# Scores and transposes on smaller tiles of the matmul array, and two weight halves loaded and split later

## The chip, the core and the metric

The kernel runs on one core of a Trainium2 chip. TensorE (PE in the profile, with its weight loads as PEld) multiplies, VectorE (DVE), ScalarE (ACT) and GpSimd (POOL) work elementwise, SyncE (SP) issues most of the DMAs. SBUF is the working memory with 128 partitions, PSUM the memory into which TensorE accumulates. The metric is the device time in microseconds, the median of the runs shown.

## The reference, cut to what matters

Three stages follow one another: a decayed linear attention, a mixture of experts with one expert for each token, and a feed-forward layer with a rational activation.

```python
def _attn_ref(q, k, v):                       # B=2, H=8, S=768, D=64
    gamma = 1.0 - 2.0 ** (-5.0 - np.arange(H)); scale = 1.0 / np.sqrt(D)
    for t in range(S):
        state = gamma[None, :, None, None] * state + np.einsum('bhd,bhe->bhde', k[:, :, t], v[:, :, t])
        y[:, :, t] = scale * np.einsum('bhd,bhde->bhe', q[:, :, t], state)

def _moe_ref(x, w_gate, w1, w2, capacity):    # x: 1536 x 512, 8 experts, hidden 1024
    logits = x @ w_gate; expert_idx = np.argmax(logits, axis=1)
    # gate_w: softmax weight of the chosen expert; each expert takes at most `capacity` tokens, in order
    h = np.maximum(np.einsum('ecd,edf->ecf', disp, w1), 0.0)
    y = np.einsum('ecf,efd->ecd', h, w2)      # out[i] = gate_w[i] * y[expert, place]

def _moe2_ref(x, w_in, w_out, a, b):          # 512 -> 2048 -> 512
    h = x @ w_in
    g = (a[0] + a[1]*h + a[2]*h**2 + a[3]*h**3) / (1 + |b[0]|*|h| + |b[1]|*h**2 + 1e-6)
    return g @ w_out
```

## The kernel before

**Attention** works on 12 units of 128 tokens (`u` = 0 to 11, six for each batch row), all eight heads of a unit at once. For one unit: `scores(u)` (L286) multiplies keys with queries into the PSUM tile `sc`, for each head a 64-row contraction that gives 128 keys x 128 queries; `mask(u)` (DVE, L294) multiplies by the causal mask into `scm`; `inter(u)` (L314) adds what the state of the earlier units gives into `yt`, as 64x64 tiles; `intra(u)` (L332) adds the masked scores times the values into the same `yt`, as 128x64 tiles; `attn_xt(u)` (DVE, L343) applies the decay and gives `xt`; `state(u)` (L300) accumulates keys times values, and ACT copies it out. `gate_mm(u)` (L352) multiplies each quarter of `xt` by the identity and the router's weights side by side (`wi`, 136 columns): that transposes 128 features into token order and gives the four parts of the logits. ACT copies the logits (`lgs`) and the tokens (`xs`), and SP stores the tokens to DRAM (`xd`). Matmuls written through `mm` have the line L341.

The loop over units (L619) writes each engine's order by hand: in a unit stand the scores of the next unit, `inter`, `intra`, `state`, and the `gate_mm` of the unit before. `sc` has one buffer, so the scores of a unit wait for the mask of the unit before.

**Routing** is done for two groups of units, 0 to 6 and 7 to 11. For the first group `gate_parts` (maximum, one-hot), `rank_mm` and `rank_pos` (places within an expert), `rank_put` (`pe`, `rr`) and `place_mm` (matmuls `tp` that put the tokens' numbers into slots) are spread over units 7 to 10, on DVE between the masks; for the second they stand behind the loop in `attn_tail` (L697), end in `indices` (`gidx`), and GpSimd then gathers the tokens of the first expert from `xd`.

**Expert weights** arrive in halves of 512 KB. A half is loaded into a raw buffer (`raw`, six of them), ACT copies it to a rounded part (`whi`, L143) and DVE forms the remainder (`wlo`, L148). Ten halves are requested inside the attention loop. Four tables (L36 to L39) say in which unit: `LOADS` the number of loads that SP issues, `HI_AT` which halves ACT copies, `LO_AT` which remainders DVE forms at a unit's start (before the mask of the next unit), `LO_END` which at its end. Halves 0 to 3 are the first expert's first layer, halves 4 to 7 its second.

**Behind the attention** the first expert works with the tokens of slot 0 already there (`early_x`, gathered by `early_gather` inside unit 10) and then with the tokens gathered last (`expert_x`, L891, matmuls `tp` at L899). Experts 1 to 7 and the feed-forward layer follow, with TensorE busy nearly throughout.

`warm` (L280) issues matmuls on zeros while TensorE has nothing to do: 7 before the first scores, 3 behind them.

Of the kernel before, what the change touches and what calls it, by code (L numbers as in the profile page):

```python
# [7 lines left out]
F32 = mybir.dt.float32  # L8
F32R = mybir.dt.float32r
# [23 lines left out]
DEC0 = 10  # L33
LAG = (2, 3, 4, 5)
WA, WC = 7, 3
LOADS = (0, 1, 0, 1, 0, 1, 0, 2, 1, 1, 1, 2)  # L36
HI_AT = {4: (0,), 5: (1,), 8: (2,), 9: (3, 4), 10: (5,)}
LO_AT = {6: (0,), 7: (1,)}
LO_END = {9: (2,), 10: (3,), 11: (4,)}  # L39
NA = 48  # L40
LOAD_AT = {1: (34, 0), 2: (34, 1), 6: (35, 0), 7: (35, 1)}
DEC_STEPS = (14, 15, 16, 17, 18, 19, 21, 22, 25, 26, 27, 28, 29, 30, 31, 33)
# [38 lines left out]
class Build:  # L81
# [198 lines left out]
    def warm(self, n, tag="tpa"):  # L280
        ps = self.bank(tag, "wp")
        for _ in range(n):
            rhs = self.wu.unsqueeze(1).to_broadcast([128, 4, 128])
            self.nc.tensor.matmul(ps, lhsT=self.wu, rhs=rhs, start=True, stop=True)

    def scores(self, u):  # L286
        kt, qt = self.feats(u)
        sc = self.sc[u] = self.pair_bank("s", "sc").rearrange("p (r j t) -> p r j t", r=2, j=4)
        for j in range(4):
            for r in range(2):  # L290
                rows = slice(64 * r, 64 * r + 64)
                self.mm(sc[:, r, j], kt[rows, j], qt[rows, j], True, True)

    def mask(self, u):  # L294
        m = self.col("mask").unsqueeze(1).to_broadcast([128, 8, 128])
# [56 lines left out]
    def gate_mm(self, u):  # L352
        nc = self.nc
        xt = self.xt.pop(u)
        if u < NU - 1:
            banks = [self.bank(t, "xk") for t in ("lg", "xk")]
        else:
            y = self.pair_bank("y", "xk")
            banks = [y[:, 0:512], y[:, 512:]]
        self.xk[u] = [b[:, 0 : 2 * 136].rearrange("p (k n) -> p k n", k=2) for b in banks]  # L360
        for k in range(4):
            nc.tensor.matmul(self.xk[u][k // 2][:, k % 2], lhsT=xt[:, k], rhs=self.wi[:, k], start=True, stop=True)
        for half in range(2):
            out = self.lgs[:, u, 2 * half : 2 * half + 2]
            nc.scalar.activation(out=out, in_=self.xk[u][half][:, :, 128:], func=AF.Copy)
# [205 lines left out]
    def attention(self):  # L571
        nc, tc, a = self.nc, self.tc, self.a
        with ExitStack() as st:
# [11 lines left out]
            self.xg0 = self.ap.tile([128, DM], F32, name="xg0")  # L585
            self.x0 = [self.ap.tile([128, 4, 128], F32R, name=n) for n in ("xh0", "xl0")]
            self.wu = self.ap.tile([128, 128], BF16, name="wu")
            nk = self.cols["gk"][0]
            self.attn_load(0, 0)
            nc.sync.dma_start(out=self.ca[:, 0:nk], in_=a["ct"][:, 0:nk])  # L590
# [11 lines left out]
            nc.sync.dma_start(out=self.ca[:, n1:], in_=a["ct"][:, n1:n0])  # L602
            dve, pool = nc.vector, nc.gpsimd
            dve.memset(self.wu, 0.0)
            dve.memset(self.ones, 1.0)
            self.warm(WA)
            self.scores(0)
# [4 lines left out]
            self.scale(1, pool)  # L612
            self.y_table(1, pool)
            self.y_table(2, pool)
            self.warm(WC)
            ident = self.col("ident").unsqueeze(1).to_broadcast([128, 4, 128])
            wg = self.col("wg").rearrange("p (k e) -> p k e", e=E)
            done = {GROUPS[b + 1] - 1: b for b in range(len(GROUPS) - 1)}
            for u in range(NU):  # L619
                last = u == NU - 1  # L620
                if u + 4 < NU:
                    for c in range(2):
                        self.attn_load(u + 4, c)
                self.load_next(LOADS[u])
                if u + 2 < NU:
                    self.scale(u + 2, pool)
                if u + 3 < UPB:
                    self.y_table(u + 3, pool)
                for n in LO_AT.get(u, ()):
                    self.split_lo(n // 2, n % 2)  # L630
# [37 lines left out]
                if u:  # L668
                    self.gate_out(u - 1, (1,))
                for n in HI_AT.get(u, ()):  # L670
                    self.split_hi(n // 2, n % 2)
                if u - 2 in done and not last:
                    self.rank_pos(done[u - 2])
                if u - 3 in done and not last:
                    self.rank_put(done[u - 3])
                for n in LO_END.get(u, ()):
                    self.split_lo(n // 2, n % 2)
# [19 lines left out]
    def attn_tail(self):  # L697
        u, b = NU - 1, len(GROUPS) - 2
        self.early_x()
        self.gate_mm(u)  # L700
        self.early_lo()
        ps = [self.pair_bank("s", "l1")[:, 0:512]]
        self.win_l1(self.x0, ps, range(0, 10))
        self.gate_group(b)
        self.gate_out(u)
        ps.append(self.pair_bank("y", "l1")[:, 0:512])
        self.load_next(4)
        self.rank_mm(b)
        self.rank_pos(b)
        self.h0 = self.wp.tile([128, 2, 512], F32, tag="wt", name="h0", bufs=3)  # L710
        self.split_hi(3, 0)
        self.win_l1(self.x0, ps, range(10, 12))
        self.win_relu(ps, self.h0, 0)
        self.split_hi(3, 1)
        self.rank_put(b)
        self.count()
        self.split_lo(2, 1)
        self.win_l1(self.x0, ps, range(12, 24))
        self.win_relu(ps, self.h0, 1)
        t0 = self.win_turn(self.h0, 0, self.bank("tpa", "htp"))  # L720
        self.place_mm(b, self.pair_bank("s", "tp"))
        t1 = self.win_turn(self.h0, 1, self.bank("st", "htp"))
        self.indices(self.gidx, E * (self.nsub + 1))
        self.split_lo(3, 0)
        self.ht0 = self.win_parts(t0)
        self.split_lo(3, 1)
        self.ht1 = self.win_parts(t1)
        self.overfull()
        self.nprep = 8
# [610 lines left out]
```

## Time and profile before

| what | value |
|---|---|
| median of 3 runs | 519.93 us (519.87 to 520.26) |
| the profiled execution | 519.19 us, of which span 517.4 us |
| TensorE busy | 504.2 us, 97% of the span |
| mean granted TensorE clock | 0.990 |
| attention loop, about | 4 to 59 us from the span's start |
| behind it to the first gathered tokens | 59 to 75 us |

A row of the timeline gives the start in us from the span's start, the time to the end of the last instruction merged into it, the engine, the line, the operation, what is written and read, the tile of the array in use (rows*columns) and the sizes; xN is the number of merged instructions. In square brackets stand the idle time of the engine before it and who ended that. Each fp32 matmul of the program shows as two passes. A pass of TensorE overlaps the next, so the difference of two starts tells what a group costs, and the length of a row is longer than that.

### The profile page before, as it was taken

How to read it: one execution, taken by the hardware profiler on the slowest of the kernel's cores; microseconds unless marked ns; L12 is line 12 of the kernel's file. 1: busy time of each engine (PE TensorE's matmuls, PEld its weight loads, DVE VectorE, ACT ScalarE, POOL GpSimd, SP SyncE). 2: the span in 40 equal slices, each digit the busy share in tenths (PEclk: the TensorE clock that was granted, in tenths of full speed). 3: DMA queues.
4: the chain of work that ended last, by engine and by line, in shares of the span. 5: the costliest groups of instructions: out<-in, count | busy, mean ns of one | idle time of the engine just before them, and what ended most of it. 6: DMA issues, size and time to landing. Idle time of an engine off the chain costs nothing.

```text
span 517.4 us, 9416 instructions
## 1 busy us (share of the span) xinstructions
PE 504.2 (97%) x3538; PEld 442.2 (85%) x3538; DVE 403.4 (78%) x578; ACT 362.0 (70%) x588; POOL 244.1 (47%) x187
## 2 busy tenths in 40 slices
PE   7999979999999999999999999999999999999995
PEld 5888857999999999999988888888888888888884
DVE  3468753897887979786596989999899998865973
ACT  1345515877685867755697989999899987776760
POOL 2531040023331548153454546776667865445775
PEclk9999989999999999999999999999999999999998
DMA  8999761989977999994310002222022200000203
GB/s 318 405 415 366 216 224 39 300 292 306 323 267 272 366 284 302 295 277 165 104 60 1 0 2 82 82 81 82 1 81 86 79 1 0 1 0 0 83 21 143
DMA packets 27554, 83.08 MB, mean 161 GB/s; under 512 B 4976, under 2 KB 5360, under 8 KB 27504
## 3 DMA queue, kind: packets, MB, share of 16 engines
q1 hardware_dynamic: 24880, 75.09, 43.0%
q0 software_dynamic: 2624, 7.35, 4.0%
q8 instruction: 28, 0.46, 0.4%
q14 instruction: 22, 0.18, 0.1%
HBM read 71.93 MB, written 10.49 MB: 159 GB/s over the span
## 4 chain that ended last, share of the span: by engine, by line
PE 64%; DVE 1%; POOL 1%; issue 1%; ACT 1%; POOLq 0%; DVEq 0%
PE h L1046 8%; PE h L1048 8%; PE h L1047 8%; PE o L1119 7%; PE o L1118 7%; PE o L1117 7%; PE l L928 3%; PE l L930 3%; PE l L957 3%; PE l L929 3%; PE l L956 3%; PE l L955 3%; POOL out L1148 1%; PE tp L899 1%; DVE fw L1083 0%
## 5 line engine op out<-in xcount | busy, mean ns | idle before, releaser
L148 DVE TENSOR_TENSOR wlo<-raw,whi 128x1024 fp32r<-128x1024 f32 x80 | 109.8, 1387 | 14.3 <-ACT whi L143 14.0
L1097 POOL TENSOR_TENSOR gg<-fx,gg 128x512 fp32r<-128x512 f32 x47 | 61.2, 1302 | 70.0 <-issue 62.2
L143 ACT ACTIVATE whi<-raw 128x1024 fp32r<-128x1024 f32 x80 | 83.2, 1055 | 3.5 <-PE l L956 3.4
L1046 PE MATMUL h<-yh,whi 128*128 128x512 f32 x192 | 74.9, 390 | 0.0
L1117 PE MATMUL o<-whi,gg 128*128 128x512 f32 x192 | 74.8, 390 | 0.0
L1047 PE MATMUL h<-yl,whi 128*128 128x512 f32 x192 | 74.7, 389 | 0.0
L1048 PE MATMUL h<-yh,wlo 128*128 128x512 f32 x192 | 74.7, 389 | 0.0
L1118 PE MATMUL o<-wlo,gg 128*128 128x512 f32 x192 | 74.7, 389 | 0.0
L1119 PE MATMUL o<-whi,gg 128*128 128x512 f32 x192 | 74.7, 389 | 0.0
L1072 POOL TENSOR_TENSOR fw<-fh,fw 128x512 f32<-128x512 f32 x48 | 64.4, 1341 | 14.6 <-ACT fw L1061 13.8
L204 POOL TENSOR_TENSOR gq<-gq 128x512 int32<-128x512 int32 x16 | 26.7, 1666 | 86.7 <-DVE gq L201 60.9
L1059 ACT ACTIVATE fx<-h,ct 128x512 f32<-128x512 f32 x48 | 37.3, 777 | 38.2 <-PE h L1048 38.1
L928 PE MATMUL l<-xh,whi 128*128 128x224 f32 x224 | 62.0, 277 | 0.1
L955 PE MATMUL l<-hh,whi 128*128 128x224 f32 x224 | 61.9, 276 | 0.0
L930 PE MATMUL l<-xh,wlo 128*128 128x224 f32 x224 | 61.5, 275 | 0.0
L957 PE MATMUL l<-hh,wlo 128*128 128x224 f32 x224 | 61.5, 274 | 0.0
L956 PE MATMUL l<-hl,whi 128*128 128x224 f32 x224 | 61.4, 274 | 0.0
L929 PE MATMUL l<-xl,whi 128*128 128x224 f32 x224 | 61.4, 274 | 0.0
L928 PEld LDWEIGHTS l<-xh,whi 128*128 128x128 f32 x224 | 43.0, 192 | 0.4 <-ACT yh L794 0.3
L956 PEld LDWEIGHTS l<-hl,whi 128*128 128x128 f32 x224 | 43.0, 192 | 0.1
L955 PEld LDWEIGHTS l<-hh,whi 128*128 128x128 f32 x224 | 43.0, 192 | 0.1
L929 PEld LDWEIGHTS l<-xl,whi 128*128 128x128 f32 x224 | 43.0, 192 | 0.0
(161 smaller groups left out, 1176.7 us busy)
## 6 DMA issues: line engine op xcount, KB each, us to landing
raw<-wm SPq DMA_DIRECT2D x64, 512.0 KB, 6.6
r<-wf SPq DMA_DIRECT2D x32, 512.0 KB, 5.0
kv<-kv SPq DMA_DIRECT2D x22, 512.0 KB, 7.3
wd<-gq SPq DMA_DIRECT2D x16, 256.0 KB, 6.2
raw<-wd SPq DMA_DIRECT2D x8, 512.0 KB, 7.0
xd<-xs SPq DMA_DIRECT2D x12, 256.0 KB, 5.5
kv<-kv SPq DMA_DIRECT2D x4, 256.0 KB, 5.0
ca<-ct SPq DMA_DIRECT2D x1, 268.0 KB, 6.0
```

The source lines that it names most:

```text
L143: nc.scalar.activation(out=self.whi[i][:, sl], in_=raw, func=AF.Copy)
L148: (eng or self.nc.vector).tensor_tensor(out=self.wlo[i][:, sl], in0=raw, in1=self.whi[i][:, sl].bitcast(F32), op=ALU.subtract)
L928: nc.tensor.matmul(ps[:, fi], lhsT=wh[:, sl], rhs=xh[:, k], start=(k == 0), stop=False)
L929: nc.tensor.matmul(ps[:, fi], lhsT=wh[:, sl], rhs=xl[:, k], start=False, stop=False)
L955: mm(lhsT=wh[:, ws], rhs=fh, start=(f == 0 and o % 2 == 0), stop=False)
L956: mm(lhsT=wh[:, ws], rhs=fo, start=False, stop=False)
L1046: nc.tensor.matmul(h, lhsT=wh[:, sl], rhs=self.yh[:, k, ts], start=(k == 0), stop=False)
L1047: nc.tensor.matmul(h, lhsT=wh[:, sl], rhs=self.yl[:, k, ts], start=False, stop=False)
L1048: nc.tensor.matmul(h, lhsT=wl[:, sl], rhs=self.yh[:, k, ts], start=False, stop=(k == 3))
L1117: self.nc.tensor.matmul(ps, lhsT=gh[:, ms], rhs=wh[:, ws], start=first, stop=False)
L1118: self.nc.tensor.matmul(ps, lhsT=gh[:, ms], rhs=wl[:, ws], start=False, stop=False)
L1119: self.nc.tensor.matmul(ps, lhsT=gl[:, ms], rhs=wh[:, ws], start=False, stop=last)
```

## The change

`scores` computes each head's 128 keys as two halves of 64, so that its tiles are 64x64 and not 64x128; the instructions double from 8 to 16 for a unit. `gate_mm` does the same with the 128 tokens of a unit: 128x64 tiles, 8 instructions and not 4. The 3 warming matmuls behind the first scores become 3 pairs on 64 rows each. In the tables, half 1 is loaded in unit 5 (before: 3), half 2 in unit 7 (5) and half 4 in unit 8 (7); the first copies of halves 1, 2, 3 and 4 move to units 7, 9, 10 and 10 (5, 8, 9 and 9), that of half 5 from unit 10 to `attn_tail`; the remainder of half 1 moves from the start of unit 7 to the start of unit 8, those of halves 2 and 3 from the ends of units 9 and 10 to the ends of 10 and 11.

```diff
-LOADS = (0, 1, 0, 1, 0, 1, 0, 2, 1, 1, 1, 2)
-HI_AT = {4: (0,), 5: (1,), 8: (2,), 9: (3, 4), 10: (5,)}
-LO_AT = {6: (0,), 7: (1,)}
-LO_END = {9: (2,), 10: (3,), 11: (4,)}
+LOADS = (0, 1, 0, 0, 0, 1, 0, 2, 2, 1, 1, 2)
+HI_AT = {4: (0,), 7: (1,), 9: (2,), 10: (3, 4)}
+LO_AT = {6: (0,), 8: (1,)}
+LO_END = {10: (2,), 11: (3, 4)}
+    def warm_pairs(self, n):
+        banks = [self.bank(t, "wp") for t in ("tpa", "st")]
+        for _ in range(n):
+            for r, ps in enumerate(banks):
+                w = self.wr[64 * r : 64 * r + 64]
+                self.mm(ps, w, w.unsqueeze(1).to_broadcast([64, 4, 128]), True, True)
     def scores(self, u):
         for j in range(4):
-            for r in range(2):
-                rows = slice(64 * r, 64 * r + 64)
-                self.mm(sc[:, r, j], kt[rows, j], qt[rows, j], True, True)
+            for c in range(2):
+                keys = slice(64 * c, 64 * c + 64)
+                for r in range(2):
+                    rows = slice(64 * r, 64 * r + 64)
+                    self.mm(sc[keys, r, j], kt[rows, j, keys], qt[rows, j], True, True)
...
         for k in range(4):
-            nc.tensor.matmul(self.xk[u][k // 2][:, k % 2], lhsT=xt[:, k], rhs=self.wi[:, k], start=True, stop=True)
+            for c in range(2):
+                toks = slice(64 * c, 64 * c + 64)
+                self.mm(self.xk[u][k // 2][toks, k % 2], xt[:, k, toks], self.wi[:, k], True, True)
...
-            self.warm(WC)
+            self.warm_pairs(WC)
...
         self.gate_mm(u)
+        self.split_hi(2, 1)
         self.early_lo()
```

TensorE's order inside a unit, from the scores of unit 4 to those of unit 5 (x8 counts the program's instructions). Before:

```order
L341 MATMUL sc<-kv 128x128 x8
L341 MATMUL yt<-kv,s 64x128 x8
L341 MATMUL yt<-scm,kv 64x128 x8
L341 MATMUL st<-kv 64x64 x8
L362 MATMUL xk<-wi,xt 128x136 x4
L341 MATMUL sc<-kv 128x128 x8
```

Now:

```order
L350 MATMUL sc<-kv 64x128 x16
L350 MATMUL yt<-kv,s 64x128 x8
L350 MATMUL yt<-scm,kv 64x128 x8
L350 MATMUL st<-kv 64x64 x8
L350 MATMUL xk<-wi,xt 64x136 x8
L350 MATMUL sc<-kv 64x128 x16
```

The order of the groups is the same; scores and `gate_mm` have twice the instructions on half the output partitions.

VectorE from unit 7 to the mask of unit 9 (`scm_634` before, `scm_748` now); the rows `lg` to `eq` are the routing of the first group, `wlo` is the remainder of half 1. Before:

```order
L148 TENSOR_TENSOR wlo_447<-raw_335,whi_446 128x1024
L298 TENSOR_TENSOR scm_566<-sc_557,ca_108 128x1024
L349 TENSOR_TENSOR xt_585<-yt_568,qd1_159 128x512
L394 TENSOR_REDUCE lg_607<-lgs_112 128x56
L395 TENSOR_REDUCE mx_608<-lg_607 128x7
L396 TENSOR_TENSOR ex_611<-lg_607,mx_608 128x56
L398 TENSOR_TENSOR eq_609<-lg_607,mx_608 128x56
L399 TENSOR_TENSOR eq_609<-eq_609,ct_61 128x56
L298 TENSOR_TENSOR scm_634<-sc_625,ca_108 128x1024
```

Now, and behind it ScalarE's rows at the same place, where the copy of half 1 (`whi_514<-raw_520`) stands:

```order
L307 TENSOR_TENSOR scm_664<-sc_647,ca_108 128x1024
L358 TENSOR_TENSOR xt_683<-yt_666,qd1_169 128x512
L405 TENSOR_REDUCE lg_709<-lgs_112 128x56
L406 TENSOR_REDUCE mx_710<-lg_709 128x7
L407 TENSOR_TENSOR ex_713<-lg_709,mx_710 128x56
L409 TENSOR_TENSOR eq_711<-lg_709,mx_710 128x56
L410 TENSOR_TENSOR eq_711<-eq_711,ct_61 128x56
L148 TENSOR_TENSOR wlo_515<-raw_520,whi_514 128x1024
L307 TENSOR_TENSOR scm_748<-sc_731,ca_108 128x1024
```

```order
L376 ACTIVATE lgs_112<-xk_696 128x16
L428 ACTIVATE xs_707<-xk_695 128x256
L408 ACTIVATE ex_713<-ex_713 128x56
L428 ACTIVATE xs_707<-xk_696 128x256
L143 ACTIVATE whi_514<-raw_520 128x1024
```

The remainder of half 1 has moved from before the mask of unit 8 to before the mask of unit 9, behind the first rows of the routing; its copy stands on ScalarE behind the exponential `ex` and the second half of `xs`.

VectorE from the end of unit 9 to the routing of the second group. Before:

```order
L492 TENSOR_TENSOR pe_772<-ct_61,pm_699 128x896
L148 TENSOR_TENSOR wlo_694<-raw_452,whi_693 128x1024
L298 TENSOR_TENSOR scm_789<-sc_780,ca_108 128x1024
L505 COPY tab_62<-tp_800 128x64
L522 TENSOR_SCALAR gidx0_76<-tab_62 128x1
L349 TENSOR_TENSOR xt_821<-yt_791,qd4_216 128x512
L148 TENSOR_TENSOR wlo_694<-raw_551,whi_693 128x1024
L349 TENSOR_TENSOR xt_868<-yt_851,qd5_278 128x512
L148 TENSOR_TENSOR wlo_768<-raw_553,whi_767 128x1024
L695 TENSOR_TENSOR xl0_115<-xtp_883,xh0_114 128x512
L394 TENSOR_REDUCE lg_908<-lgs_112 128x40
```

Now:

```order
L503 TENSOR_TENSOR pe_898<-ct_61,pm_814 128x896
L307 TENSOR_TENSOR scm_922<-sc_905,ca_108 128x1024
L516 COPY tab_62<-tp_933 128x64
L533 TENSOR_SCALAR gidx0_76<-tab_62 128x1
L358 TENSOR_TENSOR xt_954<-yt_924,qd4_238 128x512
L148 TENSOR_TENSOR wlo_894<-raw_642,whi_893 128x1024
L358 TENSOR_TENSOR xt_1008<-yt_991,qd5_312 128x512
L148 TENSOR_TENSOR wlo_894<-raw_644,whi_893 128x1024
L148 TENSOR_TENSOR wlo_984<-raw_725,whi_983 128x1024
L708 TENSOR_TENSOR xl0_115<-xtp_1028,xh0_114 128x512
L405 TENSOR_REDUCE lg_1058<-lgs_112 128x40
```

Behind `pe` the remainder of half 2 has gone; two remainders, of halves 3 and 4, stand now between the last `xt` and `xl0`, where one stood.

## Rows read from the trace of the kernel before

**Rows 1.** The page's first part: busy time, share, instructions of each engine.

```profile
PE 504.2 (97%) x3538; PEld 442.2 (85%) x3538; DVE 403.4 (78%) x578; ACT 362.0 (70%) x588; POOL 244.1 (47%) x187
```

**Rows 2.** Windows: stretch, length, busy us of each engine, granted clock, DMA.

```profile
core 0: us, PE busy (x) PEld busy (x) DVE busy (x) ACT busy (x) POOL busy (x), PEclk, DMA share, GB/s
...
40.00:53.00 13.00, 13.00 (x212) 11.61 (x212) 12.03 (x32) 6.42 (x17) 2.13 (x2) 1.00 0.93 346
...
71.40:75.00 3.60, 0.01 (x1) 0.00 (x0) 0.45 (x5) 0.00 (x0) 2.31 (x3) 0.77 0.93 315
75.00:80.20 5.20, 5.15 (x15) 4.18 (x15) 2.14 (x11) 0.49 (x1) 1.00 (x1) 0.50 0.52 184
```

**Rows 3.** Timeline of TensorE, one unit of the loop.

```profile
19.69 1.16 PE L341 MATMUL sc<-kv 64*128 64x128 f32 x16
20.78 0.67 PE L341 MATMUL yt<-kv,s 64*64 64x128 f32 x16
21.38 1.09 PE L341 MATMUL yt<-scm,kv 128*64 128x128 f32 x16
22.30 0.63 PE L341 MATMUL st<-kv 128*64 128x64 f32 x16
22.86 1.19 PE L362 MATMUL xk<-wi,xt 128*128 128x136 f32 x8
23.99 1.16 PE L341 MATMUL sc<-kv 64*128 64x128 f32 x16
```

**Rows 4.** Timeline of TensorE in narrow windows, and a group behind its like.

```profile
21.05 0.40 PE L341 MATMUL yt<-kv,s 64*64 64x128 f32 x8
...
21.16 0.29 PE L341 MATMUL yt<-kv,s 64*64 64x128 f32 x4
...
57.99 1.09 PE L362 MATMUL xk<-wi,xt 128*128 128x136 f32 x8
```

**Rows 5.** Groups by line and form, weight loads, 16 to 50 us: busy, mean ns.

```profile
L341 PEld LDWEIGHTS yt<-scm,kv 128*64 128x64 f32 x128 | 6.8, 136 | 1.3 <-issue 1.0 <-POOL kv L268 0.2
```

**Rows 6.** Timeline of TensorE, behind the first scores.

```profile
5.65 0.82 PE L284 MATMUL wp<-wu 128*128 128x512 bf16 x3
7.38 1.09 PE L341 MATMUL yt<-scm,kv 128*64 128x128 f32 x16 [0.91 <-DVE kv L268]
```

**Rows 7.** Timeline of VectorE, units 7 to 11 and behind them.

```profile
41.80 1.22 DVE L298 TENSOR_TENSOR scm<-sc,ca 128x1024 f32<-128x1024 f32 x1
...
49.23 1.08 DVE L492 TENSOR_TENSOR pe<-ct,pm 128x896 f32<-128x896 f32 x1
50.23 1.22 DVE L148 TENSOR_TENSOR wlo<-raw,whi 128x1024 fp32r<-128x1024 f32 x1
51.37 1.22 DVE L298 TENSOR_TENSOR scm<-sc,ca 128x1024 f32<-128x1024 f32 x1
...
56.64 0.69 DVE L349 TENSOR_TENSOR xt<-yt,qd 128x512 f32<-128x512 f32 x1 [1.39 <-PE yt L341]
57.25 1.22 DVE L148 TENSOR_TENSOR wlo<-raw,whi 128x1024 fp32r<-128x1024 f32 x1
59.01 0.69 DVE L695 TENSOR_TENSOR xl<-xtp,xh 128x512 fp32r<-128x512 f32 x1 [0.55 <-ACT xh L690]
```

**Rows 8.** Timeline of ScalarE, unit 7 and the copy in unit 8.

```profile
41.69 0.37 ACT L417 ACTIVATE xs<-xk 128x256 f32<-128x256 f32 x1
...
45.15 1.07 ACT L143 ACTIVATE whi<-raw 128x1024 fp32r<-128x1024 f32 x1
```

**Rows 9.** Timeline of GpSimd: values of unit 10 scaled, the first gather behind the loop.

```profile
41.70 1.09 POOL L268 TENSOR_TENSOR kv<-kv,ca 128x512 f32<-128x512 f32 x1 [3.44 <-DMA kv<-kv]
...
68.25 1.73 POOL L849 DMA_INDIRECT xg<-xd,gidx  x1 [13.86 <-DVE gidx L522]
```

**Rows 10.** Timeline of TensorE: scores of unit 10, places, first gathered tokens.

```profile
44.59 1.16 PE L341 MATMUL sc<-kv 64*128 64x128 f32 x16
...
50.58 1.77 PE L502 MATMUL tp<-rr,pe 128*128 128x64 f32 x14
...
75.05 1.09 PE L899 MATMUL tp<-ct,xg 128*128 128x128 f32 x4 [3.64 <-DMA xg<-xd,gidx]
```

More of the change, by code (lines that the diff above doesn't have):

```diff
@@ L587, in attention @@
             self.wu = self.ap.tile([128, 128], BF16, name="wu")
+            self.wr = self.ap.tile([128, 128], F32R, name="wr")
             nk = self.cols["gk"][0]
@@ L604, in attention @@
             dve.memset(self.wu, 0.0)
+            dve.memset(self.wr.bitcast(F32), 0.0)
             dve.memset(self.ones, 1.0)
```

## The prediction, made before the changed kernel ran

> **What bounds the kernel now.** I read the page's first part, then a table of windows by stage, then the timelines of TensorE, VectorE and ScalarE through the attention loop, since the change lies there alone. TensorE is busy 97% of the span [rows 1]: a time gained in the loop is kept to the end, unless another engine takes it back before the loop's work is handed on. The reader is to see two places where that can happen. In the second part of the loop, from 40 to 53 us, VectorE is busy 12.03 of 13 us beside a TensorE that is full [rows 2]: both are near their bound, and whatever is put on one of them there shows. And the loop ends in a gather: TensorE waits 3.64 us, until 75.05, for tokens whose gather GpSimd issues at 68.25, when VectorE has the indices [rows 9, 10]. So the end of the loop is not where TensorE's last group of it ends, but where VectorE's chain of routing ends. While TensorE waits the clock falls, and from 75.0 to 80.2 it is granted half [rows 2].
>
> **What the smaller tiles are worth.** A group of passes that follows one of another shape pays for it. Passes of four 64x64 tiles go in fours, 21.05 to 21.16 = 0.11 us for one round [rows 4]; the sixteen passes of `inter` would be 4 x 0.11 = 0.44 but take 20.78 to 21.38 = 0.60 [rows 3], so 0.16 is entering and leaving the shape. `gate_mm` behind another 128x128 group has a length of 1.09 and behind `state` 1.19 [rows 3, 4]: 0.10, and some 0.1 more in the start. `intra` and `state`, both 128x64, follow with nothing between.
>
> Scores and `inter` together take 19.69 to 21.38 = 1.69 us. Split in two, the scores are 32 passes, in fours 8 rounds, with `inter` 12 rounds of 0.11 in one shape: 1.31, and 0.16 for one entry and exit, 1.47. That saves 0.22. `state` and `gate_mm` take 22.30 to 23.99 = 1.69. In one shape they are 8 rounds of `state` (0.63 less one pass of 0.22, by seven steps: 0.058) = 0.47, 8 rounds of `gate_mm` in pairs (1.09 less 0.28, by seven: 0.116, the time of 136 columns at `intra`'s 0.109 for 128) = 0.93, and 0.1 of leaving: 1.49. That saves 0.20. So 0.42 for a full unit, of a period of 4.30 (19.69 to 23.99).
>
> Neither new group is in the trace, so I bound them. Dearest: scores and `inter` are 48 passes at the mean of `inter` as it is, 0.60/16 = 0.0375, 1.80 in all, a loss of 0.11 where I count a gain of 0.22. Cheapest: no entry is left anywhere, 1.69 + 1.69 - 1.31 - 1.40 = 0.67 for a unit. I take 0.42, because the steps are those of shapes that run here and only one entry of each pair goes.
>
> One rule of the Trainium skill speaks against the second group. The row first: the 64-column weight loads of `intra` take 136 ns each [rows 5], yet its 16 passes take 0.92 us in all, 21.38 to 22.30 [rows 3], so the loads lie beside passes on the same rows of the array. The Trainium skill (TensorE: Matmul & The Clock Gate, Part 3, The mechanism) says that a weight load overlaps running matmuls only when its row group differs; two 128x64 tiles share all rows. By that, the loads of the new `gate_mm` would stand bare, which is the last of the rivals; the trace of `intra` disagrees.
>
> **Where the gain goes.** Unit 6 has no `inter`, and units 0 and 1 wait on loads and VectorE. Until the logits of unit 6 are out, five pairs of scores and `inter` (5 x 0.22 = 1.1), six of `gate_mm` (6 x 0.20 = 1.2) and 0.1 of scores without `inter` have gone: 2.4 us, call it the advance. By the bounds it is 1.2 - 5 x 0.11 = 0.7 at the dearest, and 5 x 0.38 + 6 x 0.29 + 0.1 = 3.7 at the cheapest.
>
> Here the tables take it back. With them, ScalarE copies half 1 only behind the second half of unit 6's `xs`, which itself stands behind the routing's exponential. That `xs` ends at 41.69 + 0.37 = 42.06, a copy takes 1.07 [rows 8], so the remainder of half 1 can start at 43.1 of today's time; VectorE starts the mask of unit 9 at 41.80 now [rows 7], and in the new order the remainder stands ahead of it. A remainder holds VectorE for 50.23 to 51.37 = 1.14 [rows 7]. The mask then starts at 43.1 + 1.1 = 44.2, 2.4 later than now, and all of that hangs on unit 6's logits, which come the advance earlier: 2.4 - 2.4 = 0.0. Queued behind it on VectorE are the one-hot for which TensorE's rank matmuls wait, the mask of unit 10, and `pe`; in the trace they follow one another without a gap worth telling. So TensorE runs ahead and then stands, some 1.9 us before the rank matmuls and 1.1 before the place matmuls. Those start at 50.58 [rows 10] and `pe` ends at 49.23 + 1.08 = 50.31 [rows 7]: there was 0.2 of slack, they start 0.2 earlier. The removed remainder of half 2 (50.23) frees VectorE just behind that point, where nobody waits for it.
>
> From the places on TensorE leads again and saves 0.2 at one more `gate_mm` before the last `xt`: 56.64 - 0.4 = 56.2. Now two remainders follow in place of one: 0.6 + 2 x 1.14, so `xl`, which today waits for ScalarE until 59.01 [rows 7], starts at 59.1: +0.1. New entries of shape around the early tokens' transposes cost TensorE 0.1 to 0.4, beside these remainders, so nothing. Behind `xl` the routing of the second group follows on VectorE without waits that the change touches, to the indices and the gather.
>
> **The rest.** The pairs of warming matmuls stand between 5.65 and 7.38, where TensorE idles 0.91 us for VectorE [rows 6]; six passes of 0.27 serially would end at 7.3, pairs at 6.5: nothing, and up to 1.0 if the clock were still half there. Input: values of unit 10 land before 41.70, its scores run at 44.59 [rows 9, 10]; 2.9 us of slack exceed the advance, and one weight half of 512 KB less is ahead of it. SP now holds the last load of unit 11 until the remainder of half 3, with the stores of units 10 and 11 queued behind; the gather needs these, and has over 2 us. The copy of half 5 on ScalarE lies before the second exponential, in 1.2 us of idle time. Nothing.
>
> The sum at `xl`, and so at the gather, is 2.4 less the advance (0.0), less 0.2 of slack, less 0.2 of one `gate_mm`, plus 0.5 by which the second remainder outlasts the wait of today: 2.5 less the advance, +0.1, with about 0.4 of doubt in the advance. A small shift there counts in full, or by half if the clock comes back at the same moment as now, since what begins at 75.0 runs at half clock. The profiled execution, 519.19 (span 517.4 and 1.8 around it), stays 519.2 to 519.3; the median of the runs shown is 0.74 above it, so the forecast is 519.9, and the rivals are on the median's level too.
>
> **The rivals.** About 0.2% (1.0 us) is what can be told from no change.
> - Forecast, 0.58: the tables give back what the tiles gain. Its own range 519.2 to 520.8.
> - The entries vanish more fully than I count, the advance is 3.7, and the gather comes 2.5 - 3.7 = 1.2 earlier: 518.7. For it: all entries lie between shapes that differ. Against: some must remain at each of two shape changes in a unit. 0.13.
> - The clock does not fall in the wait for the gather: 5.15 us of work at half clock [rows 2] become 2.6, 517.3. Against: the wait is issue to landing of the gather, which the change leaves. 0.07; and 0.02 for other gains.
> - Slower: the fours do not hold in the scores, at the dearest bound. The advance is 0.7, the mask of unit 9 comes 1.7 late, the gather 1.8: 521.7. It decides from an advance under 1.5. For it: each query column is now read by two tiles at once; against: `inter` reads its queries in the same way. 0.09.
> - Slower: TensorE's new waits in units 8 and 9 (1.9 and 1.1 us) bring the clock down there as the wait of 3.64 did. At half for 6.8 us, as then, TensorE loses 3.4, of which its waits cover some 1.9: 521.4. Against: a wait of 0.91 at 7.38 left it whole. 0.08; and 0.01 for other losses.
> - The loads of the new `gate_mm` stand bare: 16 x 0.136 = 2.2 in place of 0.93, 1.2 for each of 12 units, less 1 that hides: 533. 0.02.
>
> With the edges of the forecast's case inside the 1.0 us: faster 0.22, same 0.58, slower 0.20. The range is 517.8 to 521.7: it takes in the forecast, the larger advance and the two slower cases of 0.09 and 0.08, and leaves out the clock's gain, the bare loads and tails, some 0.15.
>
> **What would show it.** Scores and `inter` of a unit 1.47 long, `state` and `gate_mm` 1.49, a period near 3.9 up to unit 6: the tiles are right. VectorE idle about 1.2 before the remainder of half 1, released by ScalarE's copy; the mask of unit 9 at 41.8; TensorE waiting before the rank matmuls: the tables cost what I say. The gather within 0.5 us of 68.25: the sum holds. It is wrong if the mask of unit 9 starts more than 1 us off, if the granted clock leaves 1.00 in the loop, or if scores wait for input.

## The result: slower by 0.7%

The changed kernel took 522.86 us (median of 12 runs, 520.87 to 524.36), the kernel before 519.63 beside it (12 runs): a ratio of 1.0071, 95% interval 1.0049 to 1.0092. The forecast was 519.9 with a range to 521.7, so the time lies outside it, on the slow side. The profiled run took 521.74, with a span of 520.0. Runs of one kernel differ with the granted clock over the whole span (beside the fifth to the eighth experiment the kernel before took 519.13 to 520.45 us at 0.990 and 515.94 to 517.24 at 0.999), so a time is compared by its ratio to runs beside it, and a pair of profiled runs tells where time goes and not how much.

**What is as forecast.** The tiles do what the working said. The timeline of TensorE in the changed kernel, one unit and the start of the next (start, length, engine, line, operation, out<-in, tile of the array, shape, count):

```profile
34.76 0.64 PE L350 MATMUL st<-kv 128*64 128x64 f32 x16
35.23 1.10 PE L350 MATMUL xk<-wi,xt 128*64 128x136 f32 x16
36.26 1.10 PE L350 MATMUL sc<-kv 64*64 64x128 f32 x32
37.18 0.62 PE L350 MATMUL yt<-kv,s 64*64 64x128 f32 x16
37.73 1.09 PE L350 MATMUL yt<-scm,kv 128*64 128x128 f32 x16
```

From start to start `state` and `gate_mm` take 34.76 to 36.26 = 1.50, scores and `inter` 36.26 to 37.73 = 1.47; 1.69 each before [rows 3].

**What is not.** The same engine stands in the middle of groups. The rows of its timeline at six places (in brackets: idle time, and who ended it; "issue" is nobody that the profile shows):

```profile
20.04 0.60 PE L350 MATMUL yt<-kv,s 64*64 64x128 f32 x12
21.66 0.44 PE L350 MATMUL yt<-kv,s 64*64 64x128 f32 x4 [1.02 <-issue]
...
27.77 0.39 PE L350 MATMUL st<-kv 128*64 128x64 f32 x6 [0.48 <-issue]
...
32.50 1.41 PE L350 MATMUL sc<-kv 64*64 64x128 f32 x32
...
38.65 0.28 PE L350 MATMUL st<-kv 128*64 128x64 f32 x2
40.50 0.62 PE L350 MATMUL st<-kv 128*64 128x64 f32 x14 [1.57 <-issue]
...
46.64 0.33 PE L350 MATMUL xk<-wi,xt 128*64 128x136 f32 x1 [0.71 <-issue]
...
52.94 0.54 PE L350 MATMUL sc<-kv 64*64 64x128 f32 x10 [0.26 <-issue]
```

Twelve passes of `inter`, a hole, four passes: the operands of the last four were there with those of the first. (In the scores of 32.50 the hole shows as a length of 1.41 in place of 1.10.) From the start of one pass to the start of the next the six holes take 1.29, 0.70, 0.16, 1.79, 0.99 and 0.53, 5.46 us in all (with the step of up to 0.1 us that a pass takes anyway in each). Number TensorE's instructions in the trace, each weight load, each pass and each instruction on a semaphore between them: the last one ahead of a hole has number 705, 961, 1217, 1473, 1729 and 1985, always 256 apart. The profile has two DMA queues named for instructions, and one of them, q8, has more packets when TensorE has more instructions. Its row on the page of the changed kernel (packets, MB, share of the 16 DMA engines):

```profile
q8 instruction: 31, 0.51, 0.4%
```

And on that of the kernel before (the other queue, q14, has 22 packets on both pages):

```profile
q8 instruction: 28, 0.46, 0.4%
```

Each packet is 16,384 bytes, which is 64 for each of 256 instructions. Below, for each block of 256 instructions, stand the time at which TensorE's first pass in it starts, start and end of the packet that follows, and the start of the first pass in the next block:

```
changed kernel                                   kernel before
into a block  packet          into the next      into a block  packet          into the next
 15.61        19.19 - 20.25    21.66              19.69        21.70 - 22.68    26.66
 21.66        25.51 - 26.56    27.77              26.66        28.68 - 29.72    34.55
 27.77        31.00 - 31.96    33.26              34.55        38.05 - 39.04    42.42
 33.26        38.33 - 39.28    40.50              42.42        44.94 - 46.10    49.98
 40.50        44.38 - 45.28    46.64
 46.64        49.56 - 51.55    52.94
```

Every hole ends 1.2 to 1.4 us behind the end of a packet. In the kernel before, the packets were there 3.4 to 4.8 us ahead of their use, and no hole is to be seen. The reader should take the difference from the count: a unit has 72 passes before (16 + 16 + 16 + 16 + 8) and 96 now, each with a weight load, so 256 instructions last 7 to 8 us before, and would last about 5.2 at 3.88 us a unit now; but from entering one block until the next can be used 5.5 to 7.2 us go by in the changed kernel. (An estimate for the kernel before, from the end of its packets and the 1.3 us behind it, is 4.3 to 5.8 us: its packets start 2.0 to 3.5 us behind the crossing, those of the changed kernel 2.9 to 5.1. Why they start later there is not shown.) The Trainium skill (Runtime: NRT & Kernel Launch, Instruction fetch mechanics) says that instructions are refilled in blocks of 16 KiB, 256 of them, and that a crossing is mostly hidden; the block is what the trace shows, and that it is hidden holds for the kernel before and not for the changed one.

The windows, first one of the kernel before, then those of the changed one [rows 2 has the columns]:

```profile
16.00:40.00 24.00, 24.00 (x394) 21.24 (x392) 13.67 (x14) 9.78 (x35) 9.17 (x9) 1.00 1.03 412
```

```profile
16.00:40.00 24.00, 21.43 (x494) 18.88 (x487) 12.53 (x13) 8.25 (x32) 10.11 (x9) 1.00 1.01 379
40.00:53.00 13.00, 10.83 (x254) 9.49 (x254) 9.93 (x28) 5.43 (x18) 2.09 (x2) 1.00 0.96 363
...
75.00:80.20 5.20, 2.06 (x11) 1.62 (x10) 1.20 (x7) 0.49 (x1) 3.46 (x4) 0.95 0.95 336
78.40:84.00 5.60, 5.60 (x20) 4.32 (x21) 2.14 (x11) 1.18 (x2) 1.00 (x1) 0.70 0.56 199
```

The DMA engines are as full as before up to 40 us (share 1.01, 1.03 before). TensorE, full from 16 to 53 us before, is now busy 21.43 of the first 24 us and 10.83 of the 13 behind them; what was VectorE's 12.03 is 9.93. The timeline of VectorE behind unit 6's logits shows the two losses adding up:

```profile
42.30 0.56 DVE L405 TENSOR_REDUCE lg<-lgs 128x56 f32<-128x224 f32 x1 [2.75 <-ACT lgs L376]
...
44.89 1.23 DVE L148 TENSOR_TENSOR wlo<-raw,whi 128x1024 fp32r<-128x1024 f32 x1 [0.39 <-ACT whi L143]
46.03 1.22 DVE L307 TENSOR_TENSOR scm<-sc,ca 128x1024 f32<-128x1024 f32 x1
...
53.03 1.08 DVE L503 TENSOR_TENSOR pe<-ct,pm 128x896 f32<-128x896 f32 x1
...
62.91 0.68 DVE L708 TENSOR_TENSOR xl<-xtp,xh 128x512 fp32r<-128x512 f32 x1
```

The sum over the logits (`lg`), in the kernel before

```profile
40.46 0.55 DVE L394 TENSOR_REDUCE lg<-lgs 128x56 f32<-128x224 f32 x1 [1.10 <-ACT lgs L365]
```

starts at 42.30: 1.84 late. The mask of unit 9, at 41.80 before [rows 7], starts at 46.03: 4.23 late, so 2.39 more, which is the remainder now ahead of it (1.14) and the time until ScalarE's copy of that half is there. TensorE, and then GpSimd:

```profile
47.67 0.19 PE L445 MATMUL rk<-oh,tri 128*128 128x56 bf16 x1 [0.70 <-DVE oh L413]
...
54.17 1.77 PE L513 MATMUL tp<-rr,pe 128*128 128x64 f32 x14
...
78.36 0.63 PE L913 MATMUL tp<-ct,xg 128*128 128x128 f32 x4 [3.13 <-DMA xg<-xd,gidx]
```

```profile
72.07 1.73 POOL L863 DMA_INDIRECT xg<-xd,gidx  x1 [14.19 <-DVE gidx L533]
```

Places 3.59 late, gather 3.82, first gathered tokens 3.31 [rows 9, 10]. The profiled time grew by 521.74 - 519.19 = 2.55, so 0.76 less: the clock fell again behind the wait for the gather, but 0.70 over 5.6 us now costs 1.7 where 0.50 over 5.2 us cost 2.6 [rows 2], which gives back 0.9. By the ratio the loss is 3.7 us.

### The profile page after: what moved, and what is told of

It reads as the page before. It is cut to its first block, busy times and chain, and to the rows that moved or that the text cites. A ratio compares the mean times of both kernels' runs of the same rounds, so it can differ in the third digit from the quotient of the medians.

```text
span 520.0 us, 10001 instructions
## 1 busy us (share of the span) xinstructions
PE 501.9 (97%) x3829; PEld 439.7 (85%) x3829; DVE 403.8 (78%) x579; ACT 361.9 (70%) x588; POOL 244.6 (47%) x187
## 4 chain that ended last, share of the span: by engine, by line
PE 64%; DVE 1%; POOL 1%; issue 1%; ACT 1%; POOLq 0%; DVEq 0%
PE h L1060 8%; PE h L1061 8%; PE h L1062 8%; PE o L1131 7%; PE o L1132 7%; PE o L1133 7%; PE l L942 3%; PE l L944 3%; PE l L971 3%; PE l L943 3%; PE l L970 3%; PE l L969 3%; POOL out L1162 1%; PE tp L913 1%; DVE fw L1097 0%
```

## The experiments

Two theories went in: that the supply of TensorE's instructions makes the loss (theory F below), and that the new tables do, as rivals to it. Times are medians, each with its ratio to runs of the kernel before on the same chip. That kernel itself took 518.52 us beside the first four, 518.56 beside the next four and 518.08 beside the last, less than the 519.63 from about whose level the expected times were worked out; so a range is held against the ratio times 519.63.

**The new tiles alone.** From the kernel before, only this:

```
-                self.mm(sc[:, r, j], kt[rows, j], qt[rows, j], True, True)
+            for c in range(2):
+                keys = slice(64 * c, 64 * c + 64)
...
+                    self.mm(sc[keys, r, j], kt[rows, j, keys], qt[rows, j], True, True)
...
-            nc.tensor.matmul(self.xk[u][k // 2][:, k % 2], lhsT=xt[:, k], rhs=self.wi[:, k], start=True, stop=True)
+            for c in range(2):
+                toks = slice(64 * c, 64 * c + 64)
+                self.mm(self.xk[u][k // 2][toks, k % 2], xt[:, k, toks], self.wi[:, k], True, True)
```

> The new tiles of scores and of the logits with the old tables of loads and splits (and the old warming). Theory F (TensorE's instructions come in blocks of 256, a block of 16 KB over the same DMA engines as the data, and with 96 passes of two instructions in a unit a block is used up in about 5.2 us, sooner than the next one comes): TensorE still stands inside groups of its own, with nothing released, once in every 256 of its instructions, 0.5 to 1.8 us each and some 4 to 6 us in all between 16 and 54 us; unit 6's logits come 1 to 2 us later than in the kernel before, the time is 520.2 to 522.0. Rival T (the tables did it, the tiles gain what was forecast): no such stalls, period 3.9, gather 2 us earlier, 517.0 to 517.6.

520.95 us, ratio 1.0060 (1.0040 to 1.0080), which on 519.63 is 522.7, above the range. Two of the holes on its timeline of TensorE, then places and tokens:

```profile
28.10 0.33 PE L343 MATMUL st<-kv 128*64 128x64 f32 x3 [0.61 <-issue]
...
40.80 0.50 PE L343 MATMUL st<-kv 128*64 128x64 f32 x9 [1.09 <-issue]
...
52.55 1.77 PE L506 MATMUL tp<-rr,pe 128*128 128x64 f32 x14
...
76.81 0.63 PE L903 MATMUL tp<-ct,xg 128*128 128x128 f32 x4 [3.02 <-DMA xg<-xd,gidx]
```

Five holes of 1.30, 0.83, 0.70, 1.31 and 0.81, 4.95 us in all and 256 instructions apart. (The first falls ahead of a group, at 22.11, and the profile puts it down to GpSimd's `qd`, which had ended 0.7 earlier.) Unit 6's logits are summed 2.08 late, places come 1.97 late, tokens 1.76. The tiles that were to bring the gain are slower by themselves. The rival (517.0 to 517.6) is out.

**The new tables alone.** LOADS, HI_AT, LO_AT, LO_END and the copy of half 5 in `attn_tail` from the changed kernel (three halves, 1, 2 and 4, are loaded later, not two as the title has it), the tiles of before.

> The old tiles with the new tables. Theory F: 72 passes in a unit, a block of 256 instructions lasts 7.6 us, so no stall of TensorE without a releaser; what is left is VectorE's detour (waiting 1.2 for ScalarE's copy of half 1, then 1.14 of remainder ahead of the mask of unit 9), the mask at about 44.2 in place of 41.80, gather about 2.4 later, time 521.0 to 522.2. Rival (the tables cost nothing, all of the loss is the tiles'): 519.4 to 520.0.

520.06 us, ratio 1.0043 (1.0021 to 1.0065), which on 519.63 is 521.9, inside the range expected. No hole anywhere in the loop. VectorE and then TensorE:

```profile
42.72 1.22 DVE L148 TENSOR_TENSOR wlo<-raw,whi 128x1024 fp32r<-128x1024 f32 x1 [1.16 <-ACT whi L143]
43.86 1.22 DVE L298 TENSOR_TENSOR scm<-sc,ca 128x1024 f32<-128x1024 f32 x1
```

```profile
45.77 0.19 PE L434 MATMUL rk<-oh,tri 128*128 128x56 bf16 x1 [1.58 <-DVE oh L402]
...
76.55 1.09 PE L900 MATMUL tp<-ct,xg 128*128 128x128 f32 x4 [3.00 <-DMA xg<-xd,gidx]
```

The wait of 1.16 for ScalarE's copy and the remainder are there as worked out; the sum over the logits began 0.32 earlier than before (40.14), so the mask's 43.86 is 2.4 of detour. Places come 1.67 late, the gather 2.13, tokens 1.50. With the tiles' 1.97 and 1.76 that makes 3.64 at the places and 3.26 at the tokens, where the whole change has 3.59 and 3.31: two losses side by side. (At the gather itself the two make 2.13 + 2.38 = 4.51, more than the 3.82 of the whole.)

**Half of the tiles each.** The logits alone, then the scores alone, tables of before.

> Only the logits and transposes in 128x64 tiles; scores and tables as before. 80 passes in a unit, 160 instructions of TensorE, some 4.1 us a unit, so a block of 256 lasts 6.6 us. Theory F: that is about what the next block takes to come while the DMA queues are full, so stalls of 0 to 0.5 us, under 1 us in all; time 518.4 to 519.4. Rival (a stall comes with the 128x64 shape of the logits, whatever the count): stalls as in the changed kernel, 520 to 522.

> Only the scores in 64x64 tiles; logits and tables as before. 88 passes in a unit, 176 instructions of TensorE, some 4.1 us a unit, so a block of 256 lasts 5.9 us. Theory F: stalls of 0.2 to 1 us once in 256 instructions, 1.5 to 3 us in all, which take back the 1.2 us of gain; time 519.5 to 521.0. Rival (stalls come with the shape of the scores): stalls as large as in the changed kernel, 521 to 523. Rival T: no stalls, 518.2 to 518.8.

517.99 us, ratio 1.0003 (0.9984 to 1.0023), and 518.01, 0.9998 (0.9979 to 1.0016). With the logits alone (160 instructions a unit, a block lasts some 6.6 us) there is no hole, and the first tokens come at 73.94, 1.11 early. With the scores alone (176, 5.9 us) three: 0.19, 0.46 and 0.45. The second of these on its timeline:

```profile
34.60 1.19 PE L364 MATMUL xk<-wi,xt 128*128 128x136 f32 x8 [0.24 <-issue]
```

That hole falls on a group of the old shape, so no shape of tile makes it. Tokens at 74.47, 0.58 early. With the scores alone the holes took 1.10 in all, less than the 1.5 to 3 expected; on 519.63 the ratio gives 519.5, the lower end of the range. With the logits alone it gives 519.8, above the 518.4 to 519.4 expected: what the tokens are early by isn't seen in the time. Either half alone can't be told from the kernel before; both together pass the point at which the blocks come too late.

**The holes moved.** The changed kernel with 48 instructions more ahead of the loop:

```
             self.warm_pairs(WC)
+            few = self.bank("tpa", "wp")[:, 0:8]
+            for _ in range(24):
+                nc.tensor.matmul(few, lhsT=self.wu, rhs=self.wu[:, 0:8], start=True, stop=True)
```

> The changed kernel with 24 more passes of 8 columns on TensorE behind the warming pairs, at about 7 us, so 48 instructions more ahead of everything that follows. Theory F (a block of 256 instructions): the stalls keep their distance of 256 instructions and so move 24 passes back in the program: in the unit where 12 of 16 passes of inter ran before the stall (20.04), it comes after pass 20 of 32 of the scores; where 10 of 16 of state ran (27.77), after 2 passes of intra; where 2 of 16 of state ran (40.50), after 10 of inter; where 15 of 16 of the logits ran (46.64), after 7 of state. Rival (a wait at the place: a bank, a buffer, a load of data that the trace does not name): the stalls stay at the same passes of the same groups.

TensorE's timeline:

```profile
19.83 0.87 PE L350 MATMUL sc<-kv 64*64 64x128 f32 x21
21.93 0.54 PE L350 MATMUL sc<-kv 64*64 64x128 f32 x10 [1.23 <-issue]
...
26.83 0.32 PE L350 MATMUL yt<-scm,kv 128*64 128x128 f32 x1
28.13 0.98 PE L350 MATMUL yt<-scm,kv 128*64 128x128 f32 x14 [0.97 <-issue]
...
38.81 0.60 PE L350 MATMUL yt<-kv,s 64*64 64x128 f32 x11
41.86 0.44 PE L350 MATMUL yt<-kv,s 64*64 64x128 f32 x5 [2.46 <-issue]
...
55.08 0.98 PE L350 MATMUL xk<-wi,xt 128*64 128x136 f32 x13
57.83 0.45 PE L350 MATMUL xk<-wi,xt 128*64 128x136 f32 x3 [1.77 <-issue]
```

The hole after pass 12 of `inter` is now after pass 21 of the scores (20 expected), that in `state` after the first pass of `intra` (2), that at 40.50 after pass 11 of `inter` (10). (The last two rows are the crossing that falls in the scores at 52.94 in the changed kernel.) The counter decides where TensorE stands, not the group, its bank or its data. The crossing expected in `state` behind 46.64 lies there (48.85) but without a hole: TensorE had run at a lower clock before it, and the block had lasted 7.0 us. One run, 527.12 us; what else it shows is told in the last section.

**Less traffic on the DMA engines.** The changed kernel without the first ten halves of weights:

```
+        if 2 * i + half < 10:
+            if i == half == 0:
+                self.blank = self.wp.tile([128, 1024], F32, tag="raw", name="raw", bufs=6)
+                nc.gpsimd.memset(self.blank, 0.0)
+            self.raw[i, half] = self.blank
+            return
```

> The changed kernel with the first ten halves of weights left out: they are not read from memory, a tile of zeros stands for each (so their part of the result is not computed), and 5 MB of some 13 are gone from the loop's DMA traffic; TensorE's instructions are the same. Theory F (a block comes late because its packets stand in full DMA engines): request to use falls from 6 to 7 us to 4 or 5, the stalls to under 1 us in all (5.5 in the changed kernel), a unit takes 3.9 to 4.1, unit 6's logits come 2 to 4 us earlier than in the changed kernel (42.27), the time is 517.5 to 519.5. Rival (blocks come at a rate of their own, whatever the data's traffic): stalls as before, 521 to 523.

517.49 us, ratio 0.9990 (0.9967 to 1.0013), a time that says little since work is left out. Holes of 0.92, 0.70, 0.70 and 1.24, 3.56 in all: the expectation of stalls under 1 us failed. The windows say why:

```profile
24.00:40.00 16.00, 14.67 (x334) 12.78 (x331) 9.37 (x10) 5.57 (x20) 4.18 (x4) 1.00 0.90 330
...
44.00:53.00 9.00, 6.92 (x175) 6.38 (x175) 7.57 (x23) 3.72 (x14) 1.66 (x1) 1.00 0.18 65
```

Up to 32 us the changed kernel issues only the first of these halves (at 13.0), so the edit took little from that stretch, and the DMA share up to 40 us was still 0.90: keys, queries, values and stored tokens fill the engines by themselves. Only behind 44 us was it low, and the two crossings there have no hole; but TensorE waits 2.08 for VectorE just behind the first, so this proves little. So a second run took away half of the loads of keys, queries and values as well:

```
+            if u > 4:
+                return
...
-        kt, qt = (self.kv[u][:, i].rearrange("p (j t) -> p j t", j=4) for i in range(2))
+        kt, qt = (self.kv[min(u, 4)][:, i].rearrange("p (j t) -> p j t", j=4) for i in range(2))
```

> As the run without the ten halves of weights, and from unit 5 on the keys and queries by feature are not loaded either (those of unit 4 stand for them, so the values computed are others; expert counts stay of the same size): another 3.5 MB less, so that the DMA engines are no longer full while TensorE's instructions and their number per unit stay. Theory F (a block comes late because its packets stand in full DMA engines): where the DMA share falls under 0.6, the time from crossing into a block to the start of the next transfer falls from 3 to 5 us to 0.5 to 2, and the stalls go: none over 0.3 us behind 28 us, a unit takes 3.9 us, unit 6's logits come by 39.5 (42.27 in the changed kernel). Rival (a block's transfer is asked for at a fixed time or place, and its delay has nothing to do with the data's traffic): stalls of 0.7 to 1.3 us stay as they were in the run without weights.

Its timeline of TensorE, a row of VectorE, and a window:

```profile
34.50 1.10 PE L359 MATMUL sc<-kv 64*64 64x128 f32 x32
...
38.38 1.10 PE L359 MATMUL sc<-kv 64*64 64x128 f32 x32
...
44.08 0.19 PE L454 MATMUL rk<-oh,tri 128*128 128x56 bf16 x1 [1.74 <-DVE oh L422]
...
50.57 1.77 PE L522 MATMUL tp<-rr,pe 128*128 128x64 f32 x14 [0.81 <-DVE pe L512]
```

```profile
38.72 0.55 DVE L414 TENSOR_REDUCE lg<-lgs 128x56 f32<-128x224 f32 x1 [0.92 <-ACT lgs L385]
```

```profile
24.00:40.00 16.00, 16.00 (x402) 14.40 (x396) 9.87 (x14) 6.27 (x24) 4.26 (x5) 1.00 0.58 200
```

With the DMA share at 0.58, where the changed kernel has 1.00, there is no hole in this stretch, TensorE is full, and a unit takes 38.38 - 34.50 = 3.88. A block lasts 5.3 to 5.4 us, so the instructions are used up as fast as the changed kernel would use them. Unit 6's logits are summed at 38.72. From entering a block to the start of the next packet it takes 1.5, 1.4 and less than 0 in the three crossings from 26 to 37 us, where the changed kernel has 3.2 to 5.1. So the same instructions come in time when the engines that carry them are not full. (0.58 is a mean: in the 1.5 and 1.4 us ahead of the first two packets the share was 0.86 and 0.87. What a packet waits for on these engines is not shown.) (Only the loop of this run is read: with other tokens an expert had more of them than it has places, and the kernel went through its path for that case behind the loop, 1781 us in all.)

**The detour taken out.** In the changed kernel the remainders of halves 1 and 2 moved behind the routing:

```
-LO_AT = {6: (0,), 8: (1,)}
-LO_END = {10: (2,), 11: (3, 4)}
+LO_AT = {6: (0,)}
+LO_END = {9: (1,), 10: (2,), 11: (3, 4)}
```

> The changed kernel with the remainder of half 1 moved from ahead of the mask of unit 9 to the end of unit 9's step, and that of half 2 to the end of unit 10's. The stalls of instruction supply stay (4 to 6 us in all); VectorE's detour before the mask of unit 9 goes, so that mask starts at 43.5 to 44.2 in place of 46.03, the place matmuls 1 to 2 us earlier than 54.17. Theory F with the tables' cost as a part of its own: 520.0 to 521.5, as the new tiles alone. Rival (TensorE's late passes alone set the end, the detour hides beside them): 522 to 523.

The mask of unit 9 starts at 42.64, earlier than expected, places at 53.09 (54.17 with the detour), tokens at 77.36; holes of 1.29, 0.98, 0.72, 1.26 and 1.15 stay. 521.76 us (6 runs), ratio 1.0103 (1.0061 to 1.0145) with runs from 519.17 to 526.01: above the range expected, and too wide to tell from the changed kernel's 1.0071. In the trace the detour costs 1.1 at the places, in the time it is not shown.

**A version that is slightly faster.** The tiles of the logits alone, old scores and warming, with these last tables.

> Only the logits and transposes in 128x64 tiles, old scores and warming, the new tables of loads with the remainders moved as in the run before. 160 instructions of TensorE in a unit: no stalls over 0.3 us. The mask of unit 9 at 40 to 41, gather 0.5 to 2 us earlier than in the kernel before; time 0 to 1.5 us under the kernel before. Rival (the later loads bring a wait for the second remainder at the end): 0 to 1 us over it.

517.39 us, ratio 0.9985 (0.9964 to 1.0006), no hole from 14 us to the end of the loop, tokens at 74.32, 0.73 early. Once more:

> The logits alone in 128x64 tiles with the remainders moved, once more, beside new runs of the kernel before, to tell whether it is faster than that kernel: by the first five rounds 0.9985 (0.9964 to 1.0006). If TensorE's 1.3 us in the loop are kept, 0.997 to 0.999; if what follows the gather takes them back, 0.999 to 1.001.

517.71 us, ratio 0.9984 (0.9972 to 0.9997): faster than the kernel before by about 0.16%, a size that the interval of the first five rounds alone does not tell from nothing, and than the changed one by some 0.9%. Its profile has one hole of 0.62 at 39.62, so even 160 instructions a unit are close to what the supply gives; the tokens come at 75.07 there, as before, so that the trace of this run doesn't show where the 0.16% come from (its profiled 518.37, against 519.19, goes with a granted clock of 0.67 from 75.0 to 80.2, where the kernel before had 0.50 [rows 2]).

## Why the prediction was wrong

- **Sizes of the tiles: right.** 1.47 and 1.50 against 1.47 and 1.49; a unit without holes takes 3.88 (run with half the loads) against "near 3.9". The bare weight loads of the last rival did not come: the new `gate_mm` takes 35.23 to 36.26 = 1.03, where 16 bare loads of 0.136 would take 2.2, so the loads of 128x64 tiles lie beside passes here. The Trainium skill (TensorE: Matmul & The Clock Gate, Part 3, The mechanism) lists overlap only for another row group; the trace disagrees. The same section also lets a load into the background weight buffer go ahead of running matmuls, which the prediction left out.
- **"Where the gain goes", the advance of 2.4 with bounds of 0.7 to 3.7: the step that failed.** Unit 6's logits came 1.84 late. The holes up to there are 1.29 + 0.70 + 0.16 + 1.79 = 3.94, so the tiles did gain up to 3.94 - 1.84 = 2.1 of the 2.4; freed of the holes (run with half the loads) the logits came 40.46 - 38.72 = 1.74 early, though the scores of unit 3 started 0.38 later there than in the changed kernel. Both bounds were bounds on how long passes take; that 24 passes more a unit are 48 instructions more, which have to be brought, stood nowhere in the sum. The text's own sign of being wrong shows it: the mask of unit 9 starts 4.23 off, where 1 us was the limit. What could have warned was in the trace of before: the queue of instructions, and a DMA share of 1.03 from 16 to 40 us.
- **The tables: right as a mechanism.** 2.4 of detour forecast, 2.39 and 2.4 measured; from the places to `xl` the change adds 62.91 - 59.01 - 3.59 = 0.31 (0.3 forecast). The sum "2.4 less the advance" also held where it could: freed of the holes, TensorE waits 2.01 from pass to pass before the rank matmuls and 1.08 before the places (1.9 and 1.1 forecast), and the places start at 50.57, where the kernel before had 50.58. As TensorE was itself late in the changed kernel, only 0.70 of the first wait is seen there.
- **"A small shift there counts in full, or by half": not shown.** 3.31 at the tokens became 2.55 in one pair of profiled executions, because the clock came back sooner; by the ratio it is 3.7. That the clock stays up behind the gather, a rival at 0.07, happens in executions of these very kernels: the profiled run with the detour taken out waited 3.22 us for the gather and had a clock of 0.999 over the whole span.
- **Clock in the loop, scores and input.** The granted clock stayed 1.00 up to 53 us, as forecast. The scores of unit 3 waited 0.43 for their load, another of the text's signs of being wrong; by the holes' size it hardly matters. The warming pairs moved the first `intra` from 7.38 to 7.13: nothing.
- **The rivals.** The slower case with fours that do not hold had 521.7, near the time, but by a cause that the trace denies. None of the rivals was a supply of instructions.

What stays open: what holds a packet back on the DMA engines, and why it starts later in the changed kernel than in the kernel before at the same share; what sets the 1.2 to 1.4 us between the end of a packet and the first pass that follows; and why two profiles of like kernels differ by 0.6 us in a hole.

## What to carry to other kernels

Splitting a matmul doubles its instructions: count them, two to a pass, and work out how long 256 of them last; if that comes near the time from one block to the use of the next (5.5 to 7.2 us in this loop with the DMA engines full, against 7 to 8 us that a block lasted before), expect the loop to be bound by its instructions, whatever its passes take. The sign is idle time with no releaser, inside a group, at equal counts of instructions. And of two gains that use up one reserve, one alone may be kept: logits alone and scores alone cost nothing that can be told, both together 0.6%.

## What the runs showed of the hardware

- TensorE's instructions come in packets of 16,384 bytes, which the profile counts on the same 16 DMA engines as the data, one block ahead: the next packet starts 2.0 to 5.1 us behind the crossing while the DMA share is about 1 (the changed kernel and the kernel before), and 1.5 us or less behind it at 0.58 (the run with half the loads).
- A hole can cost more than its length. In the shifted kernel TensorE stood from 39.1 to 41.86, and behind that its granted clock was near the lower of its two levels, 1.2 and 2.4 GHz (windows; one run):

```profile
44.00:46.30 2.30, 2.30 (x31) 2.03 (x28) 0.51 (x1) 0.57 (x2) 1.04 (x1) 0.54 1.02 415
46.30:50.00 3.70, 3.70 (x98) 3.51 (x96) 2.12 (x6) 2.48 (x7) 1.04 (x1) 1.00 0.74 283
```

  The next group of logits, begun at 44.41, took 1.95 in place of 1.10. The hole of 1.79 in the changed kernel, the wait of 2.01 in the run with half the loads, and one of 2.35 from pass to pass at 45.76 in the run without weights left the clock at 1.00.
- Waits of like length do not always bring the clock down: behind the wait for the gather it fell in the changed kernel (3.13 us) and not in the run with the detour taken out (3.22 us).
